# Pair 1's squares, slopes and arctan after pair 0's sine, with a table excursion of their own

## The chip, the cores and the metric

The kernel runs on one core of one Trainium2 chip. The metric is the device time of one execution in microseconds; lower is better. Three runs of the kernel before gave a median of 737.78 us (737.22 to 738.26).

## What is computed

An attention with a complex decay, then two MLPs, all in float32. The attention keeps a state of 48 x 48 for each of 2 batches and 8 heads and goes through 768 tokens:

```python
mag = np.sqrt(a_re * a_re + a_im * a_im)
scale = np.minimum(mag, 0.999) / (mag + 1e-06)
a_re_n, a_im_n = (a_re * scale, a_im * scale)
...
for t in range(S):
    ar, ai = (a_re_n[:, :, t, :, None], a_im_n[:, :, t, :, None])
    new_re = ar * S_re - ai * S_im
    new_im = ar * S_im + ai * S_re
    kv = np.einsum('bhd,bhe->bhde', k[:, :, t], v[:, :, t])
    S_re, S_im = (new_re + kv, new_im)
    y[:, :, t] = np.einsum('bhd,bhde->bhe', q[:, :, t], S_re)
```

The first MLP is a softplus between two matrices (384 to 2048 to 384), the second a mixture of four experts with relu (384 to 1024 to 384), weighted by normalised `domain_probs`.

## The kernel before

**Attention.** The 1536 tokens are twelve chunks of 128, handled as six pairs (`n` from 0 to 5; pairs 0 to 2 are batch 0). The decay is taken apart into a magnitude and an angle. For a pair, `squares` (lines 533 to 537) makes re², im² and their sum; `ratio` (539 to 546) makes 1/|re| from a logarithm and an exponential and with DVE products the slope im/re, clipped; `arctan` (555) turns it into the angle. `logmag` (548) makes the logarithm of the magnitude from the sum of squares. `prefix` (559) sums angles (what 0, tile `pf`) and log-magnitudes (what 1, tile `pl`) over a chunk with a triangular matmul; for the later pairs, POOL first adds the last row of the chunk before to the first row (line 564), which `carry` (603) brings there by two small DMAs. `wrap` (587) takes whole turns off the angle, `level` (593) copies the magnitudes, `trig` (623) makes cosine and sine. `decay` (637) scales Q and K by exponentials of the summed magnitudes, and `s3_units` (645) does the rest for a chunk: rotated Q and K (`QK`, line 655), their transposes (`tp`), scores (`sp`) with the triangular mask on DVE (`A`, line 674), the output of the chunk (`yps`), the state (`sps`, `S`) and the write of the result into `X` as a high and a low part.

**Tables.** The logarithm and the exponential are in one table set of ScalarE, arctan and sine in another. `use_table` (96) loads a set and ties the load behind the functions that used the one before; `act` ties each later function behind the load. An `excursion` (717) loads the trigonometric set, runs its parts and loads the first set again. Squares, copies, casts and absolute values need no particular set and may stand on either side of a load.

**MLPs.** Weights of the first MLP arrive as 64-bit numbers; `conv` joins their words on DVE (lines 70 to 72, tiles `fA` and `fB`), splits them into high and low parts (ACT 181, DVE 182) and stores the joined ones for the second batch. `gemm1` (line 232, tile `h`) and `third` (line 319, tile `y`) are the matmuls. The first eighth of the first MLP (`k` = 0) works on two chunks at a time, so it starts when pair 0 is finished and needs pairs 1 and 2 for its second and third block.

**Order.** The program is written as a list of small units with positions, and a scheduler that works from due times orders the instructions of every engine; each engine then runs its own list strictly in order. Only the part up to `excursion(trigs0)()` is written out directly. There pair 1's `squares` and `ratio` stand between pair 0's two chunks of magnitudes, and pair 1's `arctan` is inside pair 0's excursion:

```python
    level(0, 0)
    decay(0, 0)
    squares(1, both)
    ratio(1, both)
    level(0, 1)
    decay(0, 1)
```

Behind it, pair 1's `logmag`, its `s2_units` (prefix, wrap, level, carry), pair 2's squares and slopes and an excursion with pair 1's sines and pair 2's arctan are put at positions -8 to 0 (line 850), and pair 0's chunks at -7.9 to -3.8 (line 849).

Of the kernel before, what the change touches and what calls it, by code (L numbers as in the profile page):

```python
# [15 lines left out]
ALU = mybir.AluOpType  # L16
# [59 lines left out]
def fast_path(ctx: ExitStack, tc, bad, wsc, qkv, a_re, a_im, w_in, w_out, probs, w1, w2, out):  # L76
    nc = tc.nc
# [18 lines left out]
    def use_table(name):  # L96
        load = nc.scalar.preload_act_table_set(name)
        for i in tabs["since"]:
            behind(load, i)
        tabs["load"], tabs["since"] = load, []  # L100

    def act(out_, in_, fn, **kw):
        i = nc.scalar.activation(out_, in_, fn, **kw)  # L103
        if fn in (AF.Exp, AF.Ln, AF.Sin, AF.Arctan):
            behind(i, tabs["load"])
            tabs["since"].append(i)
        return i
# [410 lines left out]
    def wide(t, sl):  # L518
        return flat(t[:, sl, :])
# [13 lines left out]
    def squares(n, sl):  # L533
        R, I, T1, T2 = (wide(t, sl) for t in st[n])
        nc.scalar.activation(T1, R, AF.Square)
        nc.scalar.activation(T2, I, AF.Square)
        (nc.vector if n == 0 else nc.gpsimd).tensor_tensor(T2, T1, T2, ALU.add)

    def ratio(n, sl):
        R, I, T1, T2 = (wide(t, sl) for t in st[n])  # L540
        act(T1, T1, AF.Ln, bias=b_tiny)
        act(T1, T1, AF.Exp, scale=-0.5)
        nc.vector.tensor_tensor(R, R, T1, ALU.mult)
        nc.vector.scalar_tensor_tensor(R, R, 2.0, T1, ALU.subtract, ALU.mult)
        nc.vector.tensor_tensor(I, I, R, ALU.mult)
        nc.vector.tensor_scalar(I, I, SLOPE_MAX, -SLOPE_MAX, ALU.min, ALU.max)
# [8 lines left out]
    def arctan(n):  # L555
        I = wide(st[n][1], slice(0, 2))
        act(I, I, AF.Arctan)

    def prefix(n, c, what):
        cc = (CH[n] + c) % CB  # L560
        src = st[n][1 if what == 0 else 3]
        if cc > 0 and n != 0:
            row = src[0:1, c, :]
            nc.gpsimd.tensor_tensor(row, rows[0][0:1, what, :], row, ALU.add)
        ps = psum.tile([P, 512], F32, tag="a", name=f"{'pf' if what == 0 else 'pl'}{n}_{c}", bufs=3)
        if n >= 3:
            hl = att.tile([P, 2, HD], F32R, tag="dec", name=f"hl{n}_{c}_{what}")
            hi, lo = hl[:, 0, :], hl[:, 1, :]
            if what == 0:
                nc.scalar.activation(hi, src[:, c, :], AF.Copy, scale=1.0 / (2.0 * math.pi))  # L570
                nc.vector.scalar_tensor_tensor(lo, src[:, c, :], 1.0 / (2.0 * math.pi), hi.bitcast(F32),
                                               ALU.mult, ALU.subtract)
            else:
                nc.scalar.copy(hi, src[:, c, :])
                nc.vector.tensor_tensor(lo, src[:, c, :], hi.bitcast(F32), ALU.subtract)
            nc.tensor.matmul(ps[:, :HD], tri_r, hi, start=True, stop=False)
            st[n, c, what] = ps
            return nc.tensor.matmul(ps[:, :HD], tri_r, lo, start=False, stop=True)
        t, lo = ((trik, onek), (tri, ones))[what]
        prev = range(c) if n == 0 else ()  # L580
        for i in prev:
            nc.tensor.matmul(ps[:, :HD], lo, src[:, i, :], start=(i == 0), stop=False)
        mm = nc.tensor.matmul(ps[:, :HD], t, src[:, c, :], start=(len(prev) == 0), stop=True)
        st[n, c, what] = ps
        return mm

    def wrap(n, c):
        pf = st.pop((n, c, 0))
        dth = st_out(n)[0][:, c, :]
        nc.scalar.activation(dth, pf[:, :HD], AF.Identity, bias=b_magic)  # L590
        nc.vector.scalar_tensor_tensor(dth, dth, MAGIC, pf[:, :HD], ALU.subtract, ALU.subtract)

    def level(n, c):
        b, cc = (CH[n] + c) // CB, (CH[n] + c) % CB
        pl = st.pop((n, c, 1))
        dlam = st_out(n)[1][:, c, :]
        nc.scalar.copy(dlam, pl[:, :HD])
        if cc == CB - 1:
            col = stats[96:128, 2 + b:3 + b]
            nc.vector.tensor_reduce(col, dlam[96:128, :], AX.X, ALU.min)  # L600
            nc.vector.tensor_scalar(col, col, -LAM_MIN, None, ALU.add)

    def carry(n, c):
        dth, dlam = (t[:, c, :] for t in st_out(n))
        rows[0] = att.tile([1, 2, HD], F32, tag="rows", name=f"rows{n}_{c}")
        tail = att.tile([P, HD], F32, tag="tail", name=f"tail{n}_{c}")
        nc.scalar.activation(tail[96:128, :], dth[96:128, :], AF.Copy, scale=-2.0 * math.pi)
        nc.sync.dma_start(rows[0][0:1, 0, :], tail[127:128, :])
        nc.sync.dma_start(rows[0][0:1, 1, :], dlam[127:128, :])
# [13 lines left out]
    def trig(n, c=slice(0, 2)):  # L623
        Fs, Cs = wide(st_out(n)[0], c), wide(st[n][0], c)
        nc.scalar.activation(Cs, Fs, AF.Abs)
        act(Cs, Cs, AF.Sin, bias=b_hpi, scale=-TWO_PI_LO)
        act(Fs, Fs, AF.Sin, scale=TWO_PI_LO)
# [9 lines left out]
    def decay(n, c):  # L637
        qk = st["in", n, c][0]
        lam = st_out(n)[1][:, c, :]
        dec = att.tile([P, 2, HD], F32, tag="dec", name=f"dec{n}_{c}")  # L640
        act(dec[:, 0, :], lam, AF.Exp)
        act(dec[:, 1, :], lam, AF.Exp, scale=-1.0)
        nc.vector.scalar_tensor_tensor(flat(qk), flat(dec), DECAY_MAX, flat(qk), ALU.min, ALU.mult)
# [73 lines left out]
    def excursion(*parts):  # L717
        def run():
            use_table(TRIG)
            for f_ in parts:  # L720
                f_()
            use_table(LOGEXP)
        return run

    both = slice(0, 2)

    def front(n):
        return [lambda: s1_load(n), lambda: squares(n, both), lambda: ratio(n, both), excursion(lambda: arctan(n)),
                lambda: logmag(n, both)] + s2_units(n) + [excursion(lambda: trig(n))]
# [34 lines left out]
    for c in range(2):  # L764
        squares(0, one[c])
        logmag(0, one[c])
        prefix(0, c, 1)
    for c in range(2):
        ratio(0, one[c])
    level(0, 0)  # L770
    decay(0, 0)
    squares(1, both)
    ratio(1, both)
    level(0, 1)
    decay(0, 1)

    def trigs0():
        arctan(0)
        for c in range(2):
            prefix(0, c, 0)  # L780
            if c == 0:
                arctan(1)
            wrap(0, c)
            if c == 1:
                carry(0, 1)
            trig(0, one[c])

    excursion(trigs0)()

    base = [0] + [24 + 16 * i for i in range(12)]  # L790
    ring = []
# [293 lines left out]
@with_exitstack  # L1085
def attention_moe_kernel(ctx: ExitStack, tc, qkv, a_re, a_im, w_in, w_out, probs, w1, w2, v, out):
    nc = tc.nc
    top = ctx.enter_context(tc.tile_pool(name="top", bufs=1))
    bad = top.tile([1, 1], I32, name="bad")
    wsc = nc.dram_tensor("moe1_weights", (16, P, 768), F32).ap()  # L1090
    fast_path(tc, bad, wsc, qkv, a_re, a_im, w_in, w_out, probs, w1, w2, out)
    xs = nc.dram_tensor("attention_out", (NTOK, HD), F32).ap()
    flag = nc.values_load(bad[0:1, 0:1], min_val=0, max_val=1)
    with tc.If(flag > 0):
        general_path(tc, xs, v, qkv, a_re, a_im, w_in, w_out, probs, w1, w2, out)
# [53 lines left out]
```

## Time and profile before

| | |
|---|---|
| median of three runs | 737.78 us (737.22 to 738.26) |
| the profiled execution, in all | 738.36 us |
| its span, first to last instruction | 736.6 us |
| mean granted clock of TensorE | 0.988 |
| PE busy | 702.5 us (95%), 5159 matmuls |
| DVE busy | 586.4 us (80%), 1149 instructions |
| ACT busy | 487.4 us (66%), 898 instructions |
| POOL busy | 32.3 us (4%), 31 instructions |

PE is TensorE, DVE is VectorE, ACT is ScalarE, POOL is GpSimd. A timeline gives the start and the duration of each instruction in us from the start of the span, with its line, operation and tiles; in square brackets stands how long its engine had been idle and what ended that. The number behind an x says how many instructions are merged into the row.

### The profile page before, as it was taken

The page shows a single profiled execution, that of the slowest core. Times are in us where ns is not written, and L with a number is a line of the kernel's source. Part 1 is how long each engine was busy: PE and PEld are TensorE (multiplying, and loading weights), DVE is VectorE, ACT ScalarE, POOL GpSimd, SP SyncE. Part 2 cuts the span into 40 slices and gives each one's busy share as a digit, 9 for nine tenths or more (in the row PEclk, how much of TensorE's full clock was granted, in tenths as well). Part 3 has the DMA queues.
Part 4 walks back from the last instruction along what each step waited for, and adds up shares of the span by engine and source line. Part 5 has one row for each costly group of instructions (what it writes and reads, how often), then busy time and mean ns, then how long its engine had stood idle before and what let it go on. Part 6 is the DMA issues. An engine that isn't in the chain of part 4 may idle for free.

```text
span 736.6 us, 13285 instructions
## 1 busy us (share of the span) xinstructions
PE 702.5 (95%) x5159; PEld 674.9 (92%) x5159; DVE 586.4 (80%) x1149; ACT 487.4 (66%) x898; POOL 32.3 (4%) x31
## 2 busy tenths in 40 slices
PE   2789999999999999999999999999999999999996
PEld 1468899999899999999999999999999999999996
DVE  6999999955875854548888779988778898998963
ACT  7887976888896856345686665555556567766640
POOL 1122010000111001000000000000000000000000
PEclk9699999999999999999999999999999999999998
DMA  7665666621211420121022120213445345455401
GB/s 268 195 191 179 201 203 192 224 77 44 86 45 59 122 80 2 59 86 44 23 86 65 43 87 21 87 44 109 119 157 155 127 151 172 150 172 152 162 31 69
DMA packets 36342, 83.56 MB, mean 113 GB/s; under 512 B 4528, under 2 KB 13232, under 8 KB 36272
## 3 DMA queue, kind: packets, MB, share of 16 engines
q1 hardware_dynamic: 36272, 82.64, 35.5%
q8 instruction: 42, 0.69, 0.4%
q14 instruction: 28, 0.23, 0.1%
HBM read 73.95 MB, written 8.65 MB: 112 GB/s over the span
## 4 chain that ended last, share of the span: by engine, by line


## 5 line engine op out<-in xcount | busy, mean ns | idle before, releaser
L232 PE MATMUL h<-X,A 128*128 128x384 f32 (+1 forms) x936 | 175.9, 329 | 2.3 <-ACT A L181 0.8
L232 PEld LDWEIGHTS h<-X,A 128*128 128x128 f32 x936 | 153.4, 188 | 5.6 <-issue 1.6
L319 PE MATMUL y<-B,g 128*128 128x384 f32 x744 | 150.2, 335 | 0.2 <-DVE acc L350 0.2
L319 PEld LDWEIGHTS y<-B,g 128*128 128x128 f32 x744 | 131.0, 188 | 0.7 <-issue 0.5
L319 PE MATMUL y<-g,B 128*128 128x384 f32 (+1 forms) x504 | 91.0, 315 | 0.3 <-ACT g L285 0.3
L319 PE MATMUL z<-B,g 128*128 128x384 f32 x372 | 84.7, 334 | 0.0
L319 PEld LDWEIGHTS y<-g,B 128*128 128x128 f32 x504 | 79.3, 189 | 2.0 <-ACT g L285 0.6
L319 PEld LDWEIGHTS z<-B,g 128*128 128x128 f32 x372 | 66.3, 188 | 0.0
L247 ACT ACTIVATE e<-h 128x384 f32<-128x384 f32 (+1 forms) x60 | 30.8, 512 | 37.1 <-PE h L232 36.0
L250 DVE SCALAR_TENSOR_TENSOR e<-h,e 128x384 f32<-128x384 f32 (+1 forms) x60 | 34.9, 581 | 20.6 <-ACT e L103 19.8
L255 DVE SCALAR_TENSOR_TENSOR g<-h,g 128x384 fp32r<-128x384 f32 x32 | 17.7, 555 | 28.1 <-ACT g L254 28.1
L103 ACT ACTIVATE e<-e,b_one 128x384 f32<-128x384 f32 (+1 forms) x60 | 38.2, 637 | 1.3
L103 ACT ACTIVATE e<-e 128x384 f32<-128x384 f32 (+1 forms) x60 | 32.8, 547 | 1.3
L415 PE MATMUL px<-X,sA 128*128 128x384 f32 x144 | 33.4, 340 | 0.0
L319 PE MATMUL z<-g,B 128*128 128x384 f32 x144 | 32.9, 335 | 0.0
L415 PE MATMUL px<-XC,sA 128*128 128x384 f32 x144 | 32.8, 336 | 0.0
L664 PE MATMUL tp<-ident,QK 128*96 128x128 f32 x192 | 27.2, 288 | 5.7 <-DVE QK L655 4.6
L664 PEld LDWEIGHTS tp<-ident,QK 128*96 128x96 f32 x192 | 22.2, 133 | 10.3 <-DVE QK L655 6.2
L254 ACT ACTIVATE g<-h 128x384 fp32r<-128x384 f32 x32 | 15.6, 488 | 21.3 <-PE h L232 21.1
L286 DVE TENSOR_TENSOR g<-e,g 128x384 fp32r<-128x384 f32 x48 | 26.6, 555 | 3.7 <-ACT g L285 2.9
L480 ACT CAST B<-rawB 128x768 fp32r<-128x768 f32 x24 | 20.0, 834 | 14.4 <-DMA rawB<-in_w_dram 7.3
L350 DVE SCALAR_TENSOR_TENSOR acc<-y,pr,acc 128x384 f32<-128x384 f32 x46 | 26.3, 612 | 1.7 <-PE y L319 1.7
(204 smaller groups left out, 1416.7 us busy)
## 6 DMA issues: line engine op xcount, KB each, us to landing
rawA<-in_w_dram SPq DMA_DIRECT2D x32, 384.0 KB, 3.0
rawB<-in_w_dram SPq DMA_DIRECT2D x32, 384.0 KB, 3.1
rawA<-in_w_in_dram SPq DMA_DIRECT2D x16, 384.0 KB, 3.5
rawB<-in_w_out_dram SPq DMA_DIRECT2D x16, 384.0 KB, 3.8
chkw<-in_w_in_dram SPq DMA_DIRECT2D x16, 384.0 KB, 3.2
chkw<-in_w_out_dram SPq DMA_DIRECT2D x16, 384.0 KB, 3.2
qk<-in_qkv_dram SPq DMA_DIRECT2D x12, 384.0 KB, 3.4
v<-in_qkv_dram SPq DMA_DIRECT2D x12, 256.0 KB, 2.9
```

Of the source, the lines that this page charges most:

```text
L103: i = nc.scalar.activation(out_, in_, fn, **kw)
L232: nc.tensor.matmul(ps, wt[:, p, kk, o:o + P], XB[b][:, q, kk, tok], start=(n == 0), stop=(n == 3 * KT - 1))
L247: nc.scalar.activation(t, h, AF.Abs)
L250: nc.vector.scalar_tensor_tensor(t, h, 0.0, t, ALU.max, ALU.add)
L254: nc.scalar.activation(g[:, 0, :], h, AF.Relu)
L255: nc.vector.scalar_tensor_tensor(g[:, 1, :], h, 0.0, g[:, 0, :].bitcast(F32), ALU.max, ALU.subtract)
L286: nc.vector.tensor_tensor(g[:, 1, :], t, g[:, 0, :].bitcast(F32), ALU.subtract)
L319: mm = nc.tensor.matmul(ys[j], l_, r_, start=(opens and n == 0 and not mate), stop=(closes and n == 2), skip_group_check=k == 0)
L350: nc.vector.scalar_tensor_tensor(dst, ys[j], pcol, dst, ALU.mult, ALU.add)
L415: nc.tensor.matmul(ps, lt[:, p, li, :], rhs, start=(start and n == 0), stop=(stop and n == 2), skip_group_check=True)
L480: nc.scalar.copy(hi, src)
L664: nc.tensor.transpose(tp[:96, hh, :], src[:, hf * 4 + hh, :], ident)
```

## The change

Pair 1's `squares` and `ratio` move from between pair 0's two chunks to behind pair 0's excursion; pair 1's `arctan` leaves that excursion and gets one of its own behind them, with two table loads. The sum of pair 1's squares is made on DVE and no longer on POOL.

```diff
@@ squares
-        (nc.vector if n == 0 else nc.gpsimd).tensor_tensor(T2, T1, T2, ALU.add)
+        (nc.vector if n < 2 else nc.gpsimd).tensor_tensor(T2, T1, T2, ALU.add)
@@ the written-out part
     level(0, 0)
     decay(0, 0)
-    squares(1, both)
-    ratio(1, both)
     level(0, 1)
     decay(0, 1)
 
@@ trigs0
         arctan(0)
         for c in range(2):
             prefix(0, c, 0)
-            if c == 0:
-                arctan(1)
             wrap(0, c)
             if c == 1:
                 carry(0, 1)
             trig(0, one[c])
 
     excursion(trigs0)()
+    squares(1, both)
+    ratio(1, both)
+    excursion(lambda: arctan(1))()
```

The scheduler moves much more than these lines. In the excerpts the number directly behind a name's letters is the pair (`pf1`, `im1`, `t21` is the second square tile of pair 1), then comes the chunk of the pair; weights have the eighth of the work (`k`), the slice and the half; the last number is a running one.

First excerpt: PE's list from the transposes of pair 0 (`tp0`) to its scores (`sp0`). Before:

```order
L664 MATMUL tp0_0_0_229<-ident_84,QK0_0_221 96x128 x4
L664 MATMUL tp0_0_0_236<-ident_84,QK0_0_221 96x128 x4
L583 MATMUL pf1_0_243<-im1_130,trik_92 128x384
L664 MATMUL tp0_0_1_249<-ident_84,QK0_0_221 96x128 x4
L664 MATMUL tp0_0_1_256<-ident_84,QK0_0_221 96x128 x4
L664 MATMUL tp0_1_0_338<-ident_84,QK0_1_325 96x128 x4
L664 MATMUL tp0_1_0_345<-ident_84,QK0_1_325 96x128
L583 MATMUL pl1_0_246<-t21_132,tri_89 128x384
L673 MATMUL sp0_0_0_263<-qT0_0_0_228,kT0_0_0_235 128x128 x4
L673 MATMUL sp0_0_1_270<-qT0_0_1_248,kT0_0_1_255 128x128 x4
```

With the change:

```order
L664 MATMUL tp0_0_0_231<-ident_84,QK0_0_223 96x128 x4
L664 MATMUL tp0_0_0_238<-ident_84,QK0_0_223 96x128 x4
L664 MATMUL tp0_0_1_251<-ident_84,QK0_0_223 96x128 x4
L664 MATMUL tp0_0_1_258<-ident_84,QK0_0_223 96x128 x4
L664 MATMUL tp0_1_0_340<-ident_84,QK0_1_327 96x128 x4
L664 MATMUL tp0_1_0_347<-ident_84,QK0_1_327 96x128 x4
L583 MATMUL pf1_0_245<-im1_130,trik_92 128x384
L583 MATMUL pl1_0_248<-t21_132,tri_89 128x384
L673 MATMUL sp0_0_0_265<-qT0_0_0_230,kT0_0_0_237 128x128 x4
L673 MATMUL sp0_0_1_272<-qT0_0_1_250,kT0_0_1_257 128x128 x4
```

Both prefix matmuls of pair 1's first chunk stand ahead of pair 0's scores as before; the first of them (`pf1`) has gone behind all transposes that are listed, and the two now stand side by side directly ahead of the scores.

Second excerpt: ACT's list. Before, from the load that ends pair 0's excursion (`t21` holds pair 1's sum of squares, `t11` its exponentials, `im1` its slope and angle):

```order
L97 ACT_TABLE_LOAD
L103 ACTIVATE t21_132<-t21_132,b_tiny_104 128x768
L665 COPY qT0_0_0_228<-tp0_0_0_229 96x512
L103 ACTIVATE t11_131<-t21_132 128x768
L665 COPY kT0_0_0_235<-tp0_0_0_236 96x512
L665 COPY qT0_0_1_248<-tp0_0_1_249 96x512
L590 ACTIVATE im1_130<-pf1_0_243,b_magic_98 128x384
L665 COPY kT0_0_1_255<-tp0_0_1_256 96x512
L181 CAST B0_0_473<-fB0_0_0_478 128x384
L607 ACTIVATE tail1_0_329<-im1_130 32x384
L181 CAST B0_0_473<-fB0_0_1_491 128x384
L597 COPY t21_132<-pl1_0_246 128x384
```

With the change, from the load that opens pair 1's own excursion; the load that ends pair 0's, the logarithm of `t11`, a Q copy and the exponential of `t11` stand ahead of it:

```order
L97 ACT_TABLE_LOAD
L665 COPY kT0_0_0_237<-tp0_0_0_238 96x512
L665 COPY qT0_0_1_250<-tp0_0_1_251 96x512
L181 CAST B0_0_475<-fB0_0_1_493 128x384
L665 COPY kT0_0_1_257<-tp0_0_1_258 96x512
L536 ACTIVATE t22_490<-im2_488 128x768
L181 CAST A0_1_503<-fA0_1_0_508 128x384
L103 ACTIVATE im1_130<-im1_130 128x768
L97 ACT_TABLE_LOAD
L103 ACTIVATE t21_132<-t21_132,b_tiny_104 128x768
L590 ACTIVATE im1_130<-pf1_0_245,b_magic_98 128x384
L103 ACTIVATE t11_131<-t21_132 128x768
```

The logarithm and exponential of `t21` stood directly behind the load that ends pair 0's excursion; now two more loads, the arctan, pair 2's second square and two casts come between, and the rounding of `pf1` (L590) has come ahead of the exponential.

Third excerpt: DVE's list around the last masked scores of pair 2 (`A2_1_1`, second chunk, second half of the heads). Before:

```order
L72 SCALAR_TENSOR_TENSOR fB1_1_0_1485<-rawB1_1_0_1479,fB1_1_0_1485 128x384
L70 TENSOR_SCALAR fB1_1_1_1515<-rawB1_1_1_1481 128x384
L545 TENSOR_TENSOR im3_2153<-im3_2153,re3_2152 128x768
L674 TENSOR_TENSOR A2_1_1_1408<-sp2_1_1_1409,tri_89 128x512
L182 TENSOR_TENSOR B1_1_1478<-fB1_1_0_1485,B1_1_1478 128x384
L71 SCALAR_TENSOR_TENSOR fB1_1_1_1515<-rawB1_1_1_1481,fB1_1_1_1515 128x384
L70 TENSOR_SCALAR fB1_0_0_1555<-rawB1_0_0_1546 128x384
L72 SCALAR_TENSOR_TENSOR fB1_1_1_1515<-rawB1_1_1_1481,fB1_1_1_1515 128x384
L71 SCALAR_TENSOR_TENSOR fB1_0_0_1555<-rawB1_0_0_1546,fB1_0_0_1555 128x384
L712 TENSOR_TENSOR X0_119<-yps2_1_1422,X0_119 128x3x128
L182 TENSOR_TENSOR B1_1_1478<-fB1_1_1_1515,B1_1_1478 128x384
L72 SCALAR_TENSOR_TENSOR fB1_0_0_1555<-rawB1_0_0_1546,fB1_0_0_1555 128x384
```

With the change:

```order
L72 SCALAR_TENSOR_TENSOR fB1_1_1_1517<-rawB1_1_1_1483,fB1_1_1_1517 128x384
L545 TENSOR_TENSOR im3_2155<-im3_2155,re3_2154 128x768
L250 SCALAR_TENSOR_TENSOR e0_1_5_1345<-h0_1_4_1283,e0_1_5_1345 128x512
L674 TENSOR_TENSOR A2_1_0_1380<-sp2_1_0_1381,tri_89 128x512
L182 TENSOR_TENSOR B1_1_1480<-fB1_1_1_1517,B1_1_1480 128x384
L276 TENSOR_TENSOR g10_1_5_1398<-e0_1_5_1345,g00_1_5_1397 128x512
L70 TENSOR_SCALAR fB1_0_0_1557<-rawB1_0_0_1548 128x384
L70 TENSOR_SCALAR fA1_2_0_1594<-rawA1_2_0_1553 128x384
L71 SCALAR_TENSOR_TENSOR fB1_0_0_1557<-rawB1_0_0_1548,fB1_0_0_1557 128x384
L71 SCALAR_TENSOR_TENSOR fA1_2_0_1594<-rawA1_2_0_1553,fA1_2_0_1594 128x384
L674 TENSOR_TENSOR A2_1_1_1410<-sp2_1_1_1411,tri_89 128x512
```

Steps of weight conversion of the first MLP (`fB1_1_1`, `B1_1`, `fB1_0_0`, `fA1_2_0`) that stood behind the mask stand ahead of it now.

## Rows read from the trace of the kernel before

**Rows 1.** Busy time by stretch: start and end, then each engine.
```profile
core 0: us, PE busy (x) PEld busy (x) DVE busy (x) ACT busy (x) POOL busy (x), PEclk, DMA share, GB/s
60.00:70.00 10.00, 8.81 (x135) 7.28 (x124) 10.00 (x18) 5.36 (x11) 3.62 (x2) 1.00 0.51 159
100.00:120.00 20.00, 18.94 (x246) 18.01 (x245) 19.71 (x37) 11.54 (x21) 1.95 (x1) 1.00 0.64 190
120.00:150.00 30.00, 29.92 (x214) 29.07 (x213) 27.20 (x56) 25.82 (x53) 0.00 (x0) 1.00 0.63 208
```

**Rows 2.** Timeline of DVE and PE around the last mask: start us, us, engine, line.
```profile
113.33 0.69 DVE L674 TENSOR_TENSOR A<-sp,tri 128x512 f32<-128x512 f32 x1
...
114.07 0.86 PE L689 MATMUL yps<-A,v 128*32 128x128 f32 x24 [1.06 <-DVE A L674]
...
114.87 1.33 PE L232 MATMUL h<-X,A 128*128 128x256 f32 x9
```

**Rows 3.** Timeline of DVE and POOL, 10 to 15 us.
```profile
10.54 0.56 DVE L545 TENSOR_TENSOR im<-im,re 128x384 f32<-128x384 f32 x1
...
11.86 2.10 POOL L537 TENSOR_TENSOR t<-t,t 128x768 f32<-128x768 f32 x1 [10.13 <-ACT t L536]
...
12.33 2.04 DVE L545 TENSOR_TENSOR im<-im,re 128x384 f32<-128x384 f32 x1
```

**Rows 4.** Timeline of DVE: pair 1's decay product, and the pace of single forms.
```profile
52.10 0.95 DVE L643 SCALAR_TENSOR_TENSOR qk<-dec,qk 128x768 f32<-128x768 f32 x1
...
107.85 0.94 DVE L544 SCALAR_TENSOR_TENSOR re<-re,t 128x768 f32<-128x768 f32 x1
...
108.72 0.54 DVE L182 TENSOR_TENSOR A<-fA,A 128x384 fp32r<-128x384 f32 x1
...
114.40 0.56 DVE L71 SCALAR_TENSOR_TENSOR fB<-rawB,fB 128x384 int32<-128x384 int32 x1
...
114.87 0.36 DVE L70 TENSOR_SCALAR fB<-rawB 128x384 int32<-128x384 int32 x1
...
115.13 0.56 DVE L72 SCALAR_TENSOR_TENSOR fB<-rawB,fB 128x384 int32<-128x384 int32 x1
```

**Rows 5.** Timeline of ACT, 13 to 50 us.
```profile
13.99 0.94 ACT L103 ACTIVATE t<-t,b_tiny 128x768 f32<-128x768 f32 x1 [0.69 <-POOL t L537]
...
16.77 1.28 ACT L97 ACT_TABLE_LOAD   x1
...
21.43 0.84 ACT L103 ACTIVATE im<-im 128x768 f32<-128x768 f32 x1 [0.21 <-DVE im L546]
...
27.14 0.51 ACT L103 ACTIVATE t<-t 128x384 f32<-128x384 f32 x1
...
27.67 1.28 ACT L97 ACT_TABLE_LOAD   x1
...
28.96 0.94 ACT L103 ACTIVATE t<-t,b_tiny 128x768 f32<-128x768 f32 x1
...
30.27 0.84 ACT L103 ACTIVATE t<-t 128x768 f32<-128x768 f32 x1
...
48.49 0.46 ACT L711 CAST X<-yps 128x384 fp32r<-128x384 f32 x1
```

**Rows 6.** Timeline of POOL, 27 to 38 us.
```profile
27.88 1.19 POOL L564 TENSOR_TENSOR im<-rows,im 1x384 f32<-1x384 f32 x1 [13.93 <-DMA rows<-tail]
...
36.07 1.82 POOL L537 TENSOR_TENSOR t<-t,t 128x768 f32<-128x768 f32 x1 [2.30 <-ACT t L536]
```

**Rows 7.** Timeline of PE, 29 to 49 us.
```profile
29.13 1.65 PE L583 MATMUL pf<-im,trik 128*128 128x384 f32 x2 [0.78 <-POOL im L564]
...
33.82 0.91 PE L583 MATMUL pl<-t,tri 128*128 128x384 f32 x2
...
34.57 1.95 PE L673 MATMUL sp<-qT,kT 96*128 96x128 f32 x16
...
49.00 0.74 PE L232 MATMUL h<-X,A 128*128 128x256 f32 x4 [0.72 <-ACT X L711]
```

## The prediction

> **What bounds the kernel now.** I read the busy time by stretch first, then the order of instructions on ScalarE (ACT), GpSimd (POOL), TensorE (PE) and VectorE (DVE) in the first 60 us, then PE's last waits. The table by stretch [rows 1] shows two regimes. From 120 to 150 us PE has work for 29.92 of 30 us. Before that, in 60 to 70 and 100 to 120 us, it is DVE that has no free time (10.00 of 10, 19.71 of 20) while PE has gaps (8.81, 18.94); PE's last wait of this kind is the 1.06 us before the matmul at 114.07, for the last decay-masked scores (L674) of the second chunk of pair 2, which DVE started at 113.33 [rows 2]. From 114.87 PE runs without waiting. Its order from there on is the same in both programs, and so is the matmul work ahead of that point. So a shift of this mask is a shift of the end, unless PE's own work ahead of it is late for another reason. The whole question is where the front of the program puts this mask.
>
> **The sum is added on DVE.** Today POOL adds pair 1's squares from 11.86 for 2.10 us, and the DVE slope product under it takes 2.04 us where its neighbour of the same shape takes 0.56 [rows 3]: 1.48 us of DVE are lost. The change takes the POOL instruction away and puts a 768-wide add on DVE, one start later by 0.87 at the pace of such instructions (107.85 to 108.72) [rows 4]. DVE gains 1.48 - 0.87 = 0.6 us here; it is part of the account of DVE below.
>
> **What leaves the first sine's path.** ACT runs pair 1's logarithm at 13.99 today (after 0.69 idle for POOL's sum), then its exponential, then pair 0's second decays, and only then the table load at 16.77 [rows 5]. With the pair moved, those decays wait only for DVE's product with the first ones, which stands directly behind the new add and the slope product; I walk it to 14.5, the table load to 15.5, 1.3 us earlier. Pair 1's arctan (0.84, at 21.43) also leaves the path. Pair 0's last sine, which ends at 27.65 today (27.14 and 0.51), I put at 25.7: 1.9 us gained for pair 0's rotated Q and K.
>
> **What pair 1 loses.** Behind that sine comes the return load (1.28, to 27.0), the logarithm of its squares (0.94), a Q copy, the exponential (0.84, ends 29.2) [rows 5]. Then DVE's chain: three 768-wide products that wait for each other (0.95 each, [rows 4] has one), a weight instruction between them, the clip: 33.1. The second trigonometric load ends at 30.5 and is hidden by this chain and by copies that ACT makes meanwhile; the arctan stands behind a square and a cast and ends at 34.4. The load back is not hidden: 35.7. So the logarithm of the magnitude, at 28.96 today, starts near 35.75, 6.8 us later. This delay reaches pair 0 as well, since PE's order (first excerpt) has both prefix matmuls of pair 1's first chunk ahead of pair 0's scores.
>
> The way to those scores, step by step. POOL has the square sum of pair 2 (1.82) ahead of the carry add (1.19); the sum starts at 33.3 when ACT has made the second square, so the carry add ends at 36.3 [rows 6]. The prefix matmul takes between 0.9 (the second prefix now, 33.82) and 1.65 us (the first, 29.13) [rows 7]; I take the longer, since PE has idled. On ACT the rounding of that prefix is queued ahead of the exponential of the magnitude (second excerpt): the exponential ends at 39.4. DVE's log-magnitude ends at 40.7, POOL's second carry add (1.1, a little under the first in [rows 6]) at 41.8, the second prefix at 42.6. The scores start near 42.6, where they start at 34.57 today [rows 7]: **8 us late**, against 1.9 gained.
>
> From the scores to the first matmul of the first layer it takes 14.4 us today (34.57 to 49.00, [rows 7]). I walk it to 13.3 in the new order: weight conversions are out of the way, but pair 2's arctan waits for DVE's clip (47.2), and the cast of X from the second chunk now stands behind pair 1's two sines and the load back, where it stood ahead of the load, at 48.49 [rows 5]. So the first layer begins at 55.9, 6.9 us late; and DVE's decay product for pair 1 (52.10 today, [rows 4]) at 57.15, 5.05 late. One weight instruction (0.47) stands newly between it and the rotations, so the transposes of pair 1 come 5.5 late, and PE fills the time before them with the first layer's matmuls.
>
> **What comes back.** DVE did not idle meanwhile. Ahead of that decay product it has in the new order 13 instructions more than before: the add (0.87), three with the pace of L70 (0.27: 114.87 to 115.13) and nine with that of L71 (0.47: 114.40 to 114.87) [rows 4], 5.9 us in all, weight conversions that it owes anyway. So it is 5.05 late with 5.9 done, 0.86 ahead of today's account. From there to the last mask it is DVE that paces the stretch, so I count what stands ahead of the mask in its queue (third excerpt): nine instructions more, one L537, three L71, two L182 and one L72 (these six at 0.47) and two L70: 0.87 + 2.82 + 0.54 = 4.23 us, conversions for the second slice of the first MLP. The mask therefore comes 4.23 - 0.86 = **3.4 us late**, and the end with it.
>
> Bounds of this. If the conversions gave nothing back, PE's lateness at the transposes or at the first layer would stay: +5.5 to +6.9. If eight conversion steps of the last nine could be passed over, the mask would be early by the 0.86. The weight DMAs and stores move with DVE's conversions, earlier by several us on SP's queue; I cost them at nothing, since the buffers' loads land well ahead of use; if a store held an f buffer, DVE would wait at the next L70, at most one conversion of three steps, 1.2 us.
>
> Against the profiled execution (738.36 in all, span 736.6) the sum is 741.8; this execution lies 0.58 above the median of the three runs, 737.78, so the median should be **741.2**. A measurement here can tell a change from none at about 0.2%, 1.5 us.
>
> **A rule weighed.** A table load shows 1.28 us, and the next ACT instruction starts at its end: 27.67 + 1.28 = 28.95, then 28.96, and the load itself starts 0.02 after the sine's end at 27.65 [rows 5]. By the trace, then, the two added loads are 2.56 us of ACT. The Trainium skill (ScalarE: Activation LUTs, "What ACT_TABLE_LOAD costs") adds a drain of about 1.38 us to every switch of set and asks to group functions by set, which speaks against this change. As a mechanism here it would be an ACT gap around each added load; no load of this trace shows one.
>
> **The rivals.**
> 1. *Nothing comes back.* PE, not DVE, bounds the stretch after 56 us, its lateness stays. For it: PE's busy share is 18.94 of 20 in 100 to 120 us. Against: DVE's is 19.71, and PE's last gap is a wait for DVE [rows 1, 2]. +5.5 to +6.9 us: 743.3 to 744.7. Chance 0.19.
> 2. *All comes back.* At the second rotation product of pair 1's second chunk DVE's queue has nearly the same work ahead in both orders: the add and one conversion of three steps more (0.87 + 0.27 + 0.47 + 0.47 = 2.08), two small reductions, a state add and a write of X fewer (some 1.3). If the mask of pair 2 is set by the chain from there on and not by the eight conversion steps, it comes 0.8 - 0.86 later, no shift: 737.7. Chance 0.14.
> 3. *Faster.* The other side: the scores of pair 0 decide. If POOL's carry adds and ACT's second return load pass while PE still transposes pair 0 (its scores at 33 or earlier), the 1.9 us gained at pair 0's sine go through to the first layer and the end: 735.9. For it: the sine is earlier and DVE is freed of its stall. Against: the logarithm cannot start before two table loads, three dependent products and an arctan have passed, over 8 us after a sine that ends near 25.7. Scores after 34.6 decide against it. Chance 0.10.
> 4. *ACT gaps at the loads.* Two gaps ahead of pair 0's scores; with each as long as a load, 1.28, for want of a row that shows one, 2.6 more: 743.8. Chance 0.04. This is the skill's rule named above; by its figure the two drains would be 2.76 us, an estimate from that page.
>
> That the change does not do what it says is excluded by the order: two more loads stand in ACT's queue, and POOL has one instruction fewer.
>
> **How the numbers follow.** The forecast has the remaining 0.53; with 0.75 for the prefix (0.9 or 1.65), 1.2 for a conversion and 0.55 for one more DVE instruction either way, 2.5 in all, it spans 738.7 to 743.7. The range 737.0 to 745.0 takes in the forecast, rivals 1, 2 and 4, and leaves out the third and the outermost of the first. Faster by over 1.5 us: 0.10 (rival 3). Within 1.5 us: 0.18 (rival 2 and the low end of the forecast). Slower: 0.72.
>
> **What would show it.** In the changed profile: DVE's 2.04 us product back at 0.56; pair 0's table load near 15.5 and its last sine's end near 25.7; three loads between 25 and 36 us; pair 0's scores near 42; the first matmul of the first layer near 56; the decay product of pair 1 near 57; PE's last wait for a mask of pair 2 near 117.5 for 114.07, and the rest of PE's stream shifted by the same. Scores before 35 would make the chain wrong; a first layer 7 us late and an end 7 us late would make the part on what comes back wrong; an end unchanged or earlier with a late first layer would show that the eight conversion steps do not matter.

## The result and the profile after

The changed kernel takes **745.32 us** in the median (744.95 to 746.93, four runs) against 737.63 for the kernel before (four runs): ratio 1.0103, 95% interval 1.0081 to 1.0125, or 7.7 us slower. The forecast was 741.2 with a range to 745.0. The sign was right; the size was more than twice the forecast (7.7 us for 3.4), and the time lies just outside the range.

| | after |
|---|---|
| the profiled execution, in all | 744.95 us |
| its span | 743.3 us |
| mean granted clock of TensorE | 0.978 |
| PE busy | 701.4 us, 5159 matmuls |
| DVE busy | 587.7 us, 1150 instructions |
| ACT busy | 489.7 us, 900 instructions |
| POOL busy | 31.8 us, 30 instructions |

PE executes the same matmuls and is busy no longer than before; the 6.7 us of longer span are gaps. The timeline of ACT in the changed kernel (start us, us, engine, line, operation, tiles, and in brackets the idle time before and what ended it) shows the new chain, the answer to [rows 5]:

```profile
16.48 1.28 ACT L97 ACT_TABLE_LOAD   x1
...
22.19 0.52 ACT L625 ACTIVATE re<-t 128x384 f32<-128x384 f32 x1 [1.25 <-DVE t L591]
...
27.04 0.51 ACT L103 ACTIVATE t<-t 128x384 f32<-128x384 f32 x1
27.56 1.28 ACT L97 ACT_TABLE_LOAD   x1
28.86 0.94 ACT L103 ACTIVATE t<-t,b_tiny 128x768 f32<-128x768 f32 x1
...
30.17 0.84 ACT L103 ACTIVATE t<-t 128x768 f32<-128x768 f32 x1
31.02 1.28 ACT L97 ACT_TABLE_LOAD   x1
...
35.71 0.84 ACT L103 ACTIVATE im<-im 128x768 f32<-128x768 f32 x1
36.57 1.28 ACT L97 ACT_TABLE_LOAD   x1
37.86 0.93 ACT L103 ACTIVATE t<-t,b_tiny 128x768 f32<-128x768 f32 x1
...
59.19 1.28 ACT L97 ACT_TABLE_LOAD   x1
60.48 0.48 ACT L711 CAST X<-yps 128x384 fp32r<-128x384 f32 x1
60.85 0.94 ACT L103 ACTIVATE dec<-t 128x384 f32<-128x384 f32 x2
```

Pair 0's last sine ends at 27.55, where it ended at 27.65 before: nothing was gained there. Pair 1's logarithm of the magnitude starts at 37.86 and not at 28.96, and its decays (`dec`) stand behind the load at 59.19. PE, against [rows 2, 7]:

```profile
38.77 1.65 PE L583 MATMUL pf<-im,trik 128*128 128x384 f32 x2 [2.96 <-POOL im L564]
44.47 1.65 PE L583 MATMUL pl<-t,tri 128*128 128x384 f32 x2 [4.06 <-POOL t L564]
45.91 3.18 PE L673 MATMUL sp<-qT,kT 96*128 96x128 f32 x16
...
61.01 4.70 PE L232 MATMUL h<-X,A 128*128 128x256 f32 x36 [1.33 <-ACT X L711]
65.55 0.71 PE L664 MATMUL tp<-ident,QK 128*96 128x128 f32 x5
...
122.63 0.86 PE L689 MATMUL yps<-A,v 128*32 128x128 f32 x24 [0.90 <-DVE A L674]
```

Pair 0's scores are 11.3 us late (45.91 for 34.57), the first layer 12.0 (61.01 for 49.00), PE's last wait for a mask 8.56 (122.63 for 114.07). From there the shift stays: the first prefix matmul of pair 3's second chunk comes at 203.48 where it came at 194.95, 8.5 later. Behind that some 1.8 us are made up, most of it between 530 and 650 us, where two executions of one kernel differ by as much (`e12` and `e13` below).

TensorE's granted clock differs here too. It is the third number from the end of these rows, whose columns are those of [rows 1] (the first two rows are the kernel before, the last two the changed one):

```profile
30.00:40.00 10.00, 9.81 (x122) 7.45 (x120) 9.11 (x16) 8.34 (x15) 4.92 (x4) 0.85 0.73 233
40.00:50.00 10.00, 7.64 (x140) 6.01 (x139) 10.00 (x19) 9.15 (x16) 0.24 (x1) 1.00 0.49 142
```
```profile
30.00:40.00 10.00, 5.17 (x18) 3.24 (x18) 9.56 (x14) 8.46 (x12) 3.22 (x2) 0.50 0.52 176
40.00:50.00 10.00, 5.60 (x39) 4.30 (x38) 8.90 (x11) 7.17 (x11) 3.31 (x3) 0.58 0.52 158
```

In the changed kernel PE is busy for 5.2 and 5.6 of 10 us here, and the clock is at its lower level (0.50, 1.2 GHz) from 30 to 40 us and for most of the time to 50. So the second prefix takes 1.65 us where it took 0.91, and the scores 3.18 where they took 1.95. DVE, against [rows 2 to 4], with POOL:

```profile
14.01 0.55 DVE L545 TENSOR_TENSOR im<-im,re 128x384 f32<-128x384 f32 x1
...
21.34 0.36 DVE L70 TENSOR_SCALAR fB<-rawB 128x384 int32<-128x384 int32 x1 [1.10 <-DMA moe_weights<-fA]
21.61 0.55 DVE L591 SCALAR_TENSOR_TENSOR t<-t,pf 128x384 f32<-128x384 f32 x1
...
35.49 1.96 POOL L537 TENSOR_TENSOR t<-t,t 128x768 f32<-128x768 f32 x1 [33.76 <-ACT t L536]
35.84 2.02 DVE L182 TENSOR_TENSOR A<-fA,A 128x384 fp32r<-128x384 f32 x1
...
47.22 1.06 POOL L564 TENSOR_TENSOR im<-rows,im 1x384 f32<-1x384 f32 x1 [2.80 <-DMA rows<-tail]
47.36 1.35 DVE L182 TENSOR_TENSOR B<-fB,B 128x384 fp32r<-128x384 f32 x1
48.31 1.25 POOL L564 TENSOR_TENSOR t<-rows,t 1x384 f32<-1x384 f32 x1
48.63 1.75 DVE L545 TENSOR_TENSOR im<-im,re 128x768 f32<-128x768 f32 x1
50.30 1.27 DVE L674 TENSOR_TENSOR A<-sp,tri 128x512 f32<-128x512 f32 x2
...
62.06 0.94 DVE L643 SCALAR_TENSOR_TENSOR qk<-dec,qk 128x768 f32<-128x768 f32 x1
...
121.89 0.68 DVE L674 TENSOR_TENSOR A<-sp,tri 128x512 f32<-128x512 f32 x1
```

DVE waits 1.10 us at 21.34 for a store of weights to free its buffer, and pair 0's rounding (L591) is queued behind that. Pair 0's scores have ended at 49.09, but DVE comes to their masks only at 50.30: it has not been idle since 44.88, and two of its products were stretched while POOL worked. So the longer scores and the longer second prefix are hidden there and do not delay the first layer. Pair 1's decay product is 10 us late.

### The profile page after: what moved, and what is told of

Same layout as the page of the kernel before. It is cut to its first block, busy times and chain, and to the rows that moved or that the text cites. A ratio compares the mean times of both kernels' runs of the same rounds, so it can differ in the third digit from the quotient of the medians.

```text
span 743.3 us, 13288 instructions
## 1 busy us (share of the span) xinstructions
PE 701.4 (94%) x5159; PEld 676.5 (91%) x5159; DVE 587.7 (79%) x1150; ACT 489.7 (66%) x900; POOL 31.8 (4%) x30
## 4 chain that ended last, share of the span: by engine, by line
```

## Experiments

### The two halves

`e1` has only the sum on DVE, `e2` only the move.

```diff
e1, squares, from the kernel before:
-        (nc.vector if n == 0 else nc.gpsimd).tensor_tensor(T2, T1, T2, ALU.add)
+        (nc.vector if n < 2 else nc.gpsimd).tensor_tensor(T2, T1, T2, ALU.add)
e2, from the changed kernel: the same line back
```

> Only the sum of pair 1's squares goes to DVE; squares, slopes and arctan stay where the kernel before has them. Queue theory (the loss comes from pair 0's scores, which PE holds behind pair 1's two prefix matmuls, and these wait for the second excursion): pair 0's scores stay at 34 to 35 us, the 2.04 us product under POOL's sum is back near 0.56, DVE has 0.87 more to do, the end moves by -0.6 to +0.3: 737.0 to 737.9. Rival (DVE's load is what counts: the added sum pushes everything behind it): +0.9, 738.5 or more. If the sum on DVE carried the whole loss it would be 745.

> Squares, slopes and arctan move as in the change, the sum stays on POOL. Queue theory: the sum (2.1 on POOL for 0.87 on DVE) stands in the chain from pair 0's last sine to pair 1's arctan only if POOL ends it after ACT's return load; it can start when ACT has squared, earlier than that load, so the chain is as in the changed kernel: pair 0's scores at 45 to 47 us, the last mask of pair 2 near 121 to 122, 744.5 to 746. Rival (DVE's sum is the cost): near 738.

Measured: `e1` 0.9992 of before (0.9979 to 1.0006), no difference; `e2` 1.0115 (1.0099 to 1.0131), the whole loss. Pair 0's scores stand at 34.91 in `e1` and at 46.83 in `e2`. So the move makes the loss, and the sum's engine alone changes nothing that these runs show. `e2`'s last mask comes at 121.91 as expected; its median, 746.74, is 0.7 above the times expected. Of its five runs four had a mean granted clock of 0.977 to 0.980 and took 745.45 to 747.45, and one had 0.998 and took 747.29. The mean does not show the clock of the front (see the last section), so these runs do not settle what the clock costs; `e4b` below says more.

### Two loads alone

Pair 1's squares and slopes stay at their old place and only its arctan gets its own excursion.

```diff
e3b, from e1:
@@ use_table
         for i in tabs["since"]:
             behind(load, i)
+        if tabs["load"] is not None:
+            behind(load, tabs["load"])
@@ trigs0
-            if c == 0:
-                arctan(1)
@@
     excursion(trigs0)()
+    excursion(lambda: arctan(1))()
```

> Squares, sum (on DVE) and slopes of pair 1 where the kernel before has them; only its arctan leaves pair 0's excursion, for one of its own behind it. The load that opens it is tied behind the load that ends the first, so the two stand side by side; DVE's and PE's lists stay those of the kernel with the sum on DVE alone. What is added is the price of two loads, 2.56 us of ACT, against 0.84 that leaves pair 0's sine. Both theories: logarithm of the magnitude 2.0 to 2.8 late, pair 0's scores at 36.3 to 37.5, decay product of pair 1 near 54 to 55, end at 739 to 741. If the loads were the bulk of the change's price, 743 or more; if the stretch behind takes them up, 737 to 738.5.

Measured: 1.0045 (1.0029 to 1.0060), 742.57 in the median, 3.4 us more than before and above the 739 to 741 expected. ACT in `e3b`:

```profile
27.53 2.57 ACT L97 ACT_TABLE_LOAD   x2
30.11 0.84 ACT L105 ACTIVATE im<-im 128x768 f32<-128x768 f32 x1
30.97 1.28 ACT L97 ACT_TABLE_LOAD   x1
32.27 0.94 ACT L105 ACTIVATE t<-t,b_tiny 128x768 f32<-128x768 f32 x1
```

Against `e1`, whose DVE order is the same, pair 0's scores come 3.1 late (37.97 for 34.91), pair 1's decay product 3.1 (55.54 for 52.42), the last mask 3.6 (117.28 for 113.70). Nothing comes back here. So the excursion alone is some 3.5 us of the loss. The rest of the 7.7, some 4.2 us, is by subtraction the way from squares to slopes, now in series behind the sine; no run has that way alone.

Without the tie of load behind load (`e3`), the load that opens the second excursion stood at the start of ACT's list, at 0.81 us, since no function comes between the two excursions to hold it, and six more loads stood ahead of the logarithms and exponentials that followed: nine loads up to 26 us, where `e3b` has four up to 30. It took 1.0168 (1.0141 to 1.0196).

### Pair 0's scores ahead of pair 1's prefix

```diff
e4b, from the changed kernel:
-    put([lambda: logmag(1, both)] + s2_units(1) + [lambda: s1_load(2), lambda: squares(2, both), lambda: ratio(2, both)]
-        + [excursion(lambda: trig(1), lambda: arctan(2))], -8, 0)
+    put([lambda: logmag(1, both)], -8, -7.9)
+    put(s2_units(1) + [lambda: s1_load(2), lambda: squares(2, both), lambda: ratio(2, both)]
+        + [excursion(lambda: trig(1), lambda: arctan(2))], -6, -0.2)
```

> The changed kernel with the prefix units of pair 1 put later in the list (-6 to -0.2 for -7.3 to 0), so that PE has the transposes, scores, output and state of pair 0's first chunk ahead of pair 1's first prefix matmul. Second excursion, loads and DVE products are kept. Theory A (pair 0's scores, held on PE behind the two prefix matmuls, carry the loss): scores at 32 to 36 us for 45.9, first layer at 50 to 54 for 61.0, and the end follows them: 738.5 to 741.5. Theory B (pair 1's own chain carries it: slopes and arctan behind two more loads, its prefix chunks, then its sines in one excursion with pair 2's arctan, then its decays; pair 0 is a bystander): scores and first layer as early as in A, but the decay product of pair 1 still at 58 to 61 (62.06 in the changed kernel, 52.10 before), the last mask of pair 2 at 118.5 to 122, the end at 743 to 746.

Measured: 1.0140 (1.0122 to 1.0159), 749.74 in the median, slower than the change itself and than either theory allows, although the scores start at 33.62 and the first layer at 53.57. PE in `e4b`:

```profile
53.57 4.57 PE L232 MATMUL h<-X,A 128*128 128x256 f32 x36
62.70 1.70 PE L664 MATMUL tp<-ident,QK 128*96 128x128 f32 x7 [4.56 <-DVE QK L655]
```

PE does pair 0's part of the first layer in 4.57 us and then waits as long for pair 1. The decay product of pair 1 comes at 59.39, 7.3 late where the change has it 10.0 late. Theory A falls: pair 0's scores at the head of PE's queue are not what costs. The granted clock is 1.00 from 40 to 60 us here and both of pair 1's first prefixes take 0.91 us, so 7.3 us of lateness remain without the lower clock level of the changed kernel's 40 to 48 us and without the head of the queue. Theory B has this delay right but not the end: the decay product is 2.7 us earlier than in the changed kernel, and yet the last mask is 1.9 later (123.78 for 121.89). Behind PE's wait of 4.56 us the granted clock is 0.66 from 60 to 70 us (1.00 in the changed kernel), and pair 1's first 16 transposes take 3.62 us for 2.00; whether that explains all of it no run shows. (A version with the units up to 0 and not to -0.2, `e4`, took 1.0121; in it pair 1's rotation was listed ahead of its sines, so it computes something else.)

### What paces the stretch after the first layer

The forecast let DVE pace it. `e10` takes 5.3 us of weight conversions from ahead of the last mask; `e5b` lifts the wait for the store.

```diff
e10, from the changed kernel; e11, the same from the kernel before; e12, the same from e1:
-                pos, gap = 8.3 + 2.3 * n, 0.6
+                pos, gap = 14.3 + 2 * n, 0.6
e5b, from the changed kernel:
-            f = tmp.tile([P, HW], I32, tag="f", name=f"f{nm}_{h}", bufs=2)
+            f = att.tile([P, HW], I32, tag="f", name=f"f{nm}_{h}", bufs=3)
```

> The changed kernel with the weight conversions of the second slice put 6 positions later (14.3 and 2.0 apart for 8.3 and 2.3), so that DVE's list has 5.3 us less of them ahead of pair 2's last mask; up to pair 2's decay products the lists of all engines are those of the changed kernel. Theory of DVE's account: the last mask 3 to 5.3 earlier than in the changed kernel (121.89), 116.5 to 119, end 740 to 742.5. Theory of PE (PE is late from the first layer on and has only 3.0 us of idle time between there and the last mask, so nothing more can come back): mask at 120.5 to 122, end 744 to 745.5.

> The changed kernel with three buffers for the joined weights instead of two, so DVE's L70 at 21.3 us no longer waits 1.1 us for a store, and pair 0's second rounding (L591) behind it comes at once: pair 0's last sine at 26.2 to 26.6 for 27.55. Theory of the delays (the end moves by what the front loses): 743.8 to 744.5. Theory of DVE's account (the last mask comes when DVE has had its idle time and all the work that its list has ahead of it): the freed buffer lets the list pull more weight conversions ahead of that mask, 2.9 us more by the durations of the kernel before, against 1.1 us of idle time saved: the mask at 122.5 to 124, 746 to 747.5, slower than the changed kernel although the front is earlier.

Measured: `e10` 1.0114 (1.0099 to 1.0129), 746.44 in the median, no better than the change. DVE in `e10`:

```profile
117.81 0.69 DVE L674 TENSOR_TENSOR A<-sp,tri 128x512 f32<-128x512 f32 x1 [0.75 <-PE sp L673]
118.42 0.68 DVE L276 TENSOR_TENSOR g<-e,g 128x512 fp32r<-128x512 f32 x1
120.86 0.69 DVE L674 TENSOR_TENSOR A<-sp,tri 128x512 f32<-128x512 f32 x1 [1.76 <-PE sp L673]
```

Of 5.3 us less work DVE passes on 1.0 (120.86 for 121.89); now it waits for PE's scores, and between pair 1's decay product and the last mask it is idle for 5.7 us where the changed kernel has 2.1. The table by stretch, from the first layer to the last wait for a mask, shows why (the first row is the kernel before, the second the changed one):

```profile
49.00:114.07 65.07, 60.75 (x757) 54.70 (x757) 63.79 (x113) 51.77 (x93) 8.87 (x6) 1.00 0.61 191
```
```profile
61.01:122.63 61.62, 58.62 (x758) 54.43 (x758) 59.55 (x106) 48.80 (x89) 9.30 (x5) 1.00 0.59 187
```

PE executes the same number of matmuls in both, in 2.1 us less busy time in the changed kernel, and its time without work falls from 4.3 to 3.0 us: together the 3.45 us that come back. The 3.0 us left (61.62 - 58.62) are all the idle time of PE that a lighter DVE could still give back.

`e5b` took 1.0178 (1.0158 to 1.0198). Its profiled execution, 746.95, was the shortest of five. Pair 0's last load starts at 26.86 for 27.56 and the first layer at 58.74 for 61.01, but DVE has 2.9 us more conversions ahead of the mask, and PE waits there for DVE:

```profile
122.79 0.86 PE L689 MATMUL yps<-A,v 128*32 128x128 f32 x24 [1.48 <-DVE A L674]
```

So 2.3 us gained at the first layer are gone at the mask (122.05 for 121.89). The theory of DVE's account had put the mask at 122.5 to 124 and has the sign right, but the median, 751.05, is far above its 746 to 747.5. In the changed kernel DVE and PE both have hardly any slack in this stretch: take work from one and the other holds. Why `e5b`'s other runs took up to 753.7 no trace shows.

### What is left of the change, and a faster version

`e8` writes pair 1's arctan at the end of pair 0's excursion, with no load; `e11` and `e12` apply `e10`'s shift to the kernel before and to `e1`; `e13` is `e12` measured again.

```diff
e8, from e1, in trigs0:
-            if c == 0:
-                arctan(1)
...
             trig(0, one[c])
+        arctan(1)
```

> The sum on DVE, squares and slopes at their old place, and pair 1's arctan at the end of pair 0's excursion, behind the sines and not between them: no load is added. It gives pair 0's last sine 0.84 us (26.8 for 27.65) without delay for pair 1's logarithm (28.96). If pair 0's sine decided the front (what the change would buy), 736.9 to 737.5; if pair 1's chain decides, nothing moves: 737.5 to 738.5.

> The kernel before with the same shift of the second slice's conversions: 1.95 us less of them on DVE ahead of the last mask. DVE's account: mask at 111 to 112 for 113.33, end 735.5 to 737. PE theory: PE's idle time of 4.3 us ahead of that mask is not all waits for DVE; the mask comes earlier by at most the 1.06 us of its last wait, 736.7 to 738.2. If the conversions then come late for the second slice's first layer (first matmul at 133.99), a wait there takes it back or more: 738 to 741.

> The sum on DVE, everything else as in the kernel before, and the second slice's conversions put 6 positions later: 1.08 us less on DVE ahead of the last mask (0.87 for the sum, 1.95 taken away). As for the kernel before with that shift, within 0.5 us of it: 735.5 to 738.2; this is the half of the change that costs nothing, joined with the shift.

> The kernel of the run before (the sum on DVE, the second slice's conversions 6 positions later) measured once more against the kernel before. Its front showed no shift at the later marks (the first prefix matmul of the third batch pair at 194.98 for 194.95), so if its lead of 0.19% came from the front it was chance: 0.9985 to 1.001. If the different order of the conversions gives something in the later stretches, 0.997 to 0.9985 again.

`e8` 0.9997 (0.9985 to 1.0009) and `e11` 1.0002 (0.9992 to 1.0012): no difference. But `e8` does not do what was meant. The scheduler put the arctan back between pair 0's sines, and up to 60 us ACT's list is that of `e1`:

```profile
21.35 0.83 ACT L103 ACTIVATE im<-im 128x768 f32<-128x768 f32 x1
22.32 0.52 ACT L625 ACTIVATE re<-t 128x384 f32<-128x384 f32 x1
```

So `e8` repeats `e1`, and what an earlier place for the sines buys was not tested by it. `e12` 0.9981 (0.9971 to 0.9991), `e13` 0.9968 (0.9953 to 0.9984): the sum on DVE with later conversions beats the kernel before in both measurements, by 1.3 and 2.2 us in the medians. Part of the gain can be seen from the first layer to the last mask: 62.9 us in `e12` (50.14 to 113.07) and 62.6 in `e13` (48.88 to 111.45), against 64.3 before, 64.4 in `e1` and 63.5 in `e11`. In `e12`'s profile the first layer starts 1.1 us late, so the first prefix matmul of pair 3's second chunk is where it was (194.98 for 194.95); in `e13`'s it is 1.3 earlier (193.7). How much of the medians' gain this is stays open, since between 530 and 650 us single executions differ by more than that.

## Why the prediction was wrong

The step that failed is the walk of the front, from the table load ahead of pair 0's sines through pair 1's chain to the first layer and to pair 1's decay product: put at 6.9 and 5.05 us late, measured at 12.0 and 10.0. The chain was the right one, and this term of the sum was about half its true size.

- **The sum on DVE**: right as to the product, which takes 0.55 us now (14.01); `e1` shows no change of the time, and the forecast 0.6 us in DVE's account is too small for its interval.
- **"I put at 25.7: 1.9 us gained"**: wrong. The sine ended at 27.55. The table load came at 16.48 for the 15.5 walked; the last of pair 0's squares had started at 6.68 for 5.74 before, since its data came late. Then came the wait for the store, named in the prediction and costed at nothing: 1.10 us, with pair 0's rounding queued behind it. `e5b`, without that wait, gives back 0.7 us at this sine.
- **Pair 1's delay**: the steps were right and each came late by what the sine hadn't gained, and more: arctan's end 36.55 for 34.4, logarithm 37.86 for 35.75, scores 45.91 for 42.6. Beyond the 1.85 of the sine, 0.75 is the second prefix (1.65 for the 0.9 taken): the 0.9 was read at 33.82 in a kernel whose clock was up again by then, and here PE was still at its lower level. This 0.75 is hidden again behind DVE at the masks. The rest is spread over POOL's and ACT's steps.
- **"The first layer begins at 55.9, 6.9 us late"**: 61.01, 12.0 late. Of the 5.1 us between, 3.3 are the scores' lateness. The walk from scores to first layer took 15.1 us for 13.3, and 1.6 of these 1.8 us are two DVE products under POOL's carry adds (1.35 for 0.55 at L182, 1.75 for 0.95 at L545), ahead of the masks; the cast of X came behind the sines and the load, as foreseen. The decay product was put 5.05 late and came 10.0 late; in `e4b` 7.3 us of this remain though pair 0's first scores are out of its way on PE. What pair 0's work on DVE and ACT adds to these 7.3 no run separates.
- **"3.4 us late, and the end with it"**: from first layer to last mask 3.45 us came back (12.0 to 8.56), and 3.5 were forecast (6.9 to 3.4). In this order of work the account of DVE holds: with the measured lateness of the decay product, 10.0 for 5.05, it gives 10.0 - 5.9 + 4.23 = 8.3 us at the mask, and 8.56 were measured. What it lacks is PE. `e10` shows that less work on DVE does not bring the mask forward by as much, since PE takes over after 1.0 us. Rival 1 named that engine, but its "nothing comes back" is wrong by 3.45 us, and its price was too low because the first layer's lateness was.
- **What bounds the kernel**: DVE's 19.71 of 20 us against PE's 18.94 [rows 1] was read as one engine that paces and one that follows. A stretch in which two engines are 95% and 99% busy has little room to take up a delay on either, and in the changed kernel both are busy for 20.00 of these 20 us.
- **ACT gaps at the loads** (rival 4): excluded. After each load the next ACT instruction starts 0.01 to 0.02 us later, and `e3b`'s two loads side by side take 2.57 us.
- **The range**: it was said to leave out the outermost of rival 1, but 744.7 lies inside 737.0 to 745.0.

With the measured lateness of the decay product the forecast's own sum would have been 741.2 + 4.9 = 746.1, for 745.32 measured.

## What to carry to other kernels

Before a stage is moved behind another, walk the whole chain of the moved one to the next engine that will starve for it, and put a price on each wait for a buffer on that way: here a wait of 1.10 us for a store held the rounding queued behind it, and without it (`e5b`) pair 0's last sine came 0.7 us earlier. What can come back later is bounded by the idle time of every busy engine in the stretch that has to take it up, not by the account of the busiest one. Moving a wait off the head of one queue (`e4b`) gains nothing if the engine then runs out of work for the same late producer.

## What was not expected of the hardware

A DVE instruction stretches while POOL works in many places, not only at the one that the change removes: at 35.84 a 128x384 product took 2.02 us, under POOL's 1.96 us sum from 35.49, where its form takes 0.56. The stretched products that are shown end nearly the same time after POOL's instruction: those of 384 columns 0.41 to 0.43 us (14.37 for 13.96 before; 37.86 for 37.45 and 48.71 for 48.28 now), that of 768 columns 0.82 (50.38 for 49.56). So a carry add of a single row, 1.06 to 1.25 us long, stretches DVE's products as a sum over 128 rows does. Moving one sum from POOL to DVE removes one such place and leaves the others.

A mean granted clock near 1 does not show that the front ran at the higher level. `e12`'s profiled execution has a mean of 0.998, and still its first prefix of pair 1 takes what it takes at the lower level, and the one at 40.36 half of that:

```profile
29.52 1.65 PE L583 MATMUL pf<-im,trik 128*128 128x384 f32 x2 [1.19 <-POOL im L564]
...
40.36 0.81 PE L583 MATMUL pf<-im,trik 128*128 128x384 f32 x2
```

Its trace has no record of the clock before some 35 us, and time without a record counts as 1.00. So that two runs of the kernel before took the same time, 737.32 at 0.998 and 737.39 at 0.990 (beside `e5b`), does not show that the clock of the front is free.
